# A new order table for a fused attention and channel-mix kernel, with one-bank tiles for the first transposes and the reciprocal as an operation of its own

## The chip, the cores and the metric

The kernel runs on one core of a Trainium2 chip. The core has TensorE (matmuls and transposes), VectorE, ScalarE, GpSimd and SyncE, each with an instruction queue of its own that is worked in order; they wait for one another by semaphores. TensorE writes to PSUM, eight banks here of 128 partitions x 512 float32; the other engines copy from there to SBUF. Transfers are issued here by GpSimd (loads of inputs and weights, which cast float32 to bfloat16 on the way) and by SyncE (stores, and transposes from SBUF to SBUF). The metric is the device time of one execution in microseconds. Before the change the median of three runs is 307.29 us (306.47 to 307.72).

## The reference

Two layers in a row. First an attention with a feature map, for 8 batches of 8 heads, 576 positions and a head size of 64:

```python
def phi(x):
    proj = np.einsum('bhsd,df->bhsf', x, w_phi)                  # 64 -> 128 features
    proj = proj - np.max(np.abs(proj), axis=-1, keepdims=True)
    return np.concatenate([np.exp(proj), np.exp(-proj)], axis=-1)
q_p, k_p = (phi(q), phi(k))
kv = np.einsum('bhsf,bhsd->bhfd', k_p, v)
z = np.sum(k_p, axis=2)
num = np.einsum('bhsf,bhfd->bhsd', q_p, kv)
den = np.einsum('bhsf,bhf->bhs', q_p, z)[..., None] + 1e-06
attn = num / den
```

Then, with the heads side by side as x (8 x 576 x 512), a channel mix of a batch's row with the row before it:

```python
x_prev = np.concatenate([np.zeros((B, 1, D)), x[:, :-1, :]], axis=1)
xk = mu_k * x + (1.0 - mu_k) * x_prev
xr = mu_r * x + (1.0 - mu_r) * x_prev
k = np.maximum(xk @ w_k, 0.0)                                    # 512 -> 1024
v = k * k @ w_v                                                  # 1024 -> 512
r = 1.0 / (1.0 + np.exp(-(xr @ w_r)))
out = r * v
```

## The kernel before

The kernel works in "pairs": two heads of one batch, numbered 0 to 31, four to a batch. Every step of a pair or a batch is an entry in a plan, with a name; a long text, ORDER, says in which order the entries are written into the program. As every engine works in order, this text fixes the order on each engine. An entry may carry the number of its PSUM buffer (`:1`), the engine that does it (`/ACT`), and filler matmuls ahead of it (`+3@0`: three, into buffer 0), which keep TensorE going. Entries that end in `.d` mark the landing of a transfer and write nothing into the program.

```python
ORDER = """
ones ident lv0.0 lv0.0.d:0 lk0.1 lq0.1 lv0.1 dve2 hk hq hk.d:0 lk0.1.d:0 dve3 hq.d:0 lk0.0.d/ACT
lq0.0.d/DVE lk0.2 lq0.2 pt0:2+9@0 wphi wphi.d:0 mus dve1 lv0.2 lk1.0 pb0/DVE pa0/ACT tr0 tp0.0:2+1@0
# ... (some hundred lines)
```

PSUM is shared out as three double buffers P0 to P2 of two banks each and two single ones, M0 and M1:

```python
def fill(n, i):
    t = psum.tile([128, 512], FP, name="ps_f", tag=f"M{i}")
    for _ in range(n):
        nc.tensor.matmul(t, lhsT=ones[:, 0:128], rhs=ones, start=True, stop=True)

def ptile(key, name):
    return psum.tile([128, 2, 512], FP, name=name, tag=f"P{plan.place[key]}")

def motile(key, name):
    return psum.tile([128, 512], FP, name=name, tag=f"M{plan.place[key]}")
```

Queries and keys are loaded by GpSimd (`lk`, `lq`; values: `lv`; weights: `wk`, `wr`, `wv`) and transposed: those of the first two batches (pairs 0 to 7) by TensorE (`pt`, then copies `pa` and `pb`), those of the others by a DMA transpose of SyncE (`tr`).

```python
def pt(b, a):
    def f():
        # ...
        ps = ptile(("P", f"pt{i}"), "ps_pt")
        pb = ps.rearrange("p a x -> p (a x)").bitcast(BF).rearrange("p (a g t) -> p a g t", a=2, t=128)
        st["pb", i] = pb
        for g in range(R):                                        # R = 9
            bk, o = divmod(g, 5)
            nc.tensor.transpose(pb[:, bk, o, :], nat[b][:, a, g * 128:(g + 1) * 128], ident)
    return f

def tr(p0, p1):
    def f():
        # ...
        nc.sync.dma_start_transpose(out=t[:, R * p0:R * p1, :],
                                    in_=nat[b][:, p0:p1, :].rearrange("p a x -> p (a x)"))
    return f
```

A pair n then goes: projections of queries and keys (`qp`, `kp`), the greatest absolute values (`rq`, `rk`: tile `nm`), these split in two bfloat16 parts on GpSimd (`mh`: tile `mhl`), transposed (`mt`, `mc`) and added back by a matmul (`ka`, and in `qt` for queries), exponentials (`ea`, `eb`, `qa`, `qb`), the product of keys and values (`kv`, `kc`), numerator and denominator (`nd`), division (`rd`). The last positions of all pairs of a batch go a way of their own by parts of a batch (`tp`, `rt`, `mhe`: tile `mhlt`, `mte`, `mce`, `kae`, `ekt`, `qte`, `eqe`). The division and what follows:

```python
def rd():
    s["rd"] = small.tile([128, 2, 5], FP, name="rden")
    ndv = s["nd"][:, :, 0:325].rearrange("p b (s e) -> p b s e", e=65)
    nc.vector.reciprocal(s["rd"], ndv[:, :, :, 64])
    s["x"] = mid.tile([128, 10, 64], BF, name="x_sc", bufs=BUFS["x"])
    nc.vector.tensor_tensor(s["x"].rearrange("p (b s) d -> p b s d", b=2), ndv[:, :, :, 0:64],
                            s["rd"].to_broadcast([128, 2, 5, 64]), op=ALU.mult)

def xz():                                                         # pairs 8 to 31
    newx()
    nc.sync.dma_start_transpose(out=xs[:, a, :].rearrange("p (g t) -> p g t", g=5),
                                in_=s["x"].rearrange("p s d -> p (s d)"))

def xu(eng):                                                      # the edge copy
    copy(eng, xs[:, a, 1:64], xs[:, a, 576:639])
    (nc.vector if eng == "DVE" else nc.gpsimd).memset(xs[:, a, 0:1], 0.0)
```

For pairs 0 to 7 TensorE transposes the result instead (`xt`, copies `xe` and `xf`). Then come the difference of neighbours (`df`, on VectorE or GpSimd) and the two mixes (`xa`, `xb`, on VectorE). With the four pairs of a batch b mixed, its channel mix follows: `h` (into 1024), `rl` (relu), `sq` (square), `r` and `th` (the gate), `v` and `ob` (product), `so` (store); the last positions of two batches go together (`he`, `re`, `ve`, ...). The matmuls of `h`, `r` and `v` stand between those of the pairs of later batches.

Of the kernel before, what the change touches and what calls it, by code (L numbers as in the profile page):

```python
# [19 lines left out]
ones ident lv0.0 lv0.0.d:0 lk0.1 lq0.1 lv0.1 dve2 hk hq hk.d:0 lk0.1.d:0 dve3 hq.d:0 lk0.0.d/ACT  # L20
lq0.0.d/DVE lk0.2 lq0.2 pt0:2+9@0 wphi wphi.d:0 mus dve1 lv0.2 lk1.0 pb0/DVE pa0/ACT tr0 tp0.0:2+1@0
rt0.0 mhe0.0 lk0.2.d:0 qp0:1 rq0 lq0.2.d:0 kp0:0 rk0 mte0.0:1+3@0 lq1.0 lq1.0.d:0 lv1.0 mh0
lq0.1.d:0 pt1:1 pa1/DVE mce0.0/ACT kae0.0 lk1.2 lq1.2 lv1.2 pb1/ACT tr1 lq1.2.d:0 qp1:1+2@0 mt0:1
rq1 ekt0.0 mc0/ACT wk.0 pt2:2 ka0 pb2/DVE pa2/ACT kp1:1 rk1 mh1 ea0 pt3:2 pb3/ACT lk1.0.d:0 eb0
pa3/DVE tr3 mt1:1+4@0 mc1/DVE tr2 vc0/POOL wk.1 qp2:2 ka1 ea1 mus.d:0 eb1 rq2 kv0:0 kc0/DVE wr.0
wk.1.d:0 wr.1 lv1.2.d:0 kp2:2+1@0 rk2 wv.0 qt0:0 pt4:1+1@0 lv1.0.d:0 mh2 mt2:1+1@0 qa0 qb0 lk1.2.d:0
pa4/DVE pb4/DVE qte0.0:0 eqe0.0 tp0.1:1 mc2/DVE ka2 tr4 lv0.2.d:0 pt5:0 ea2 rt0.1 mhe0.1
mte0.1:0+1@1 pb5/DVE wv.0.d:0 pa5/DVE eb2 mce0.1/DVE kae0.1+2@1 lv0.1.d:0 ekt0.1 pt6:0 pb6/ACT
pa6/DVE pt7:2 pa7/DVE nd0:1 qt1:0 rd0 pb7/ACT vc1/POOL vc2/POOL vc3/ACT qp3:2 rq3 kp3:1+1@1 wv.1 rk3
mh3 tr6 qa1 qb1 tp0.2:2+3@1 qte0.1:0 tr7 eqe0.1 rt0.2 mhe0.2 kv1:0 kc1/ACT xt0:1 xf0/ACT mt3:0  # L30
mc3/ACT nd1:0 tr5 vc4/POOL xe0/ACT ka3 ea3 eb3 df0/POOL mte0.2:1+1@0 rd1 xt1:0 mce0.2/DVE kae0.2
ekt0.2 tp1.0:0 qte0.2:1 eqe0.2 rt1.0 qp4:1 qt2:2 lk2.0 qa2 qb2 mhe1.0 mte1.0:1 rq4 xa0 kv2:1 kc2/ACT
mce1.0/DVE kae1.0 ekt1.0 vc5/POOL xf1/DVE xb0 qte1.0:1 wr.0.d:0 kp4:2 kv3:1 eqe1.0 kc3/ACT nd2:0 rk4
mh4 mt4:1 rd2 qp5:1 mc4/ACT ka4 rq5 xe1/ACT wk.0.d:0 ea4 eb4 lq2.0 xt2:1 lq2.0.d:0 qp6:0 rq6
df1/POOL xa1 qt3:1+1@0 qa3 kv4:2+1@0 kc4/DVE wk.d xb1 wr.1.d:0 kp5:0 qt4:2+1@0 rk5 qb3 nd3:1 rd3 mh5
xe2/ACT mt5:0+3@0 lk2.0.d:0 tr2.0 xf2/ACT xt3:1 qa4 qb4 mc5/ACT df2/DVE ka5 xe3/ACT xf3/ACT tr2.2
xa2 xb2 wv.1.d:0 ea5 eb5 nd4:2 rd4 df3/POOL xa3 qt5:1 qa5 xb3 kv5:0+3@0 tr2.2.d:0 kp6:2 xt4:1
xf4/ACT xe4/DVE kc5/ACT h0.0:0 h0.1:1 qb5 rl0.0/ACT rl0.1/ACT sq0.0/ACT vc6/POOL vc7/DVE rk6 qp7:1
nd5:0 df4/POOL rq7 mh6 mt6:1 mc6/ACT h0.2:0 rl0.2/ACT qt6:1 qa6 xa4 tr2.0.d:0 wr.d r0.0:1 tr9 xb4
sq0.2/POOL th0.0 tr8 rd5 h0.3:0 qb6 sq0.1/POOL rl0.3/DVE lv2.0 lv2.0.d:0 xt5:1 xf5/DVE xe5/DVE ka6  # L40
kp7:0 h0.4:0 h0.5:1 qp8:1 ea6 df5/POOL eb6 rl0.4/ACT sq0.4/ACT rk7 mh7 sq0.3/ACT kv6:2 rl0.5/DVE
mt7:1 mc7/ACT lk3.0 lq3.0 lv3.0 lk4.0 lq4.0 rq8 lk4.0.d:0 kc6/ACT r0.1:0 th0.1 ka7 ea7 eb7 tr11 tr10
lq3.0.d:0 tp2.0:1 rt2.0 h0.6:1 r0.2:0 rl0.6/DVE sq0.6/ACT th0.2 nd6:2 rd6 h0.7:1 mhe2.0 mte2.0:0
mce2.0/DVE vc8/POOL vc9/POOL kv7:0 kc7/DVE rl0.7/ACT vc10/POOL kae2.0 ekt2.0 qp9:2 rq9 qte2.0:1
xt6:0 sq0.7/POOL qt7:0 lk3.0.d:0 xf6/DVE xe6/DVE eqe2.0 qa7 qb7 kp8:1 rk8 kp9:2 rk9 wv.d sq0.5/POOL
v0.0:0 ob0.0 tr3.0 so0.0 mh8 mt8:1 nd7:0 mc8/ACT ka8 mh9 mt9:0 mc9/ACT xa5 tr3.2 xb5 v0.1:1 rd7
ob0.1 tr3.2.d:0 vc11/ACT ea8 df6/POOL eb8 xa6 xb6 v0.2:0 ob0.2 xt7:1 xe7/ACT xf7/ACT qt8:1 qa8 qb8
df7/DVE xa7 xb7 ka9 lv3.0.d:0 vc12/POOL kv8:0 r0.3:0 tr3.0.d:0 tr13 tr12 lq4.0.d:0 th0.3 v0.3:1
kc8/DVE ob0.3 kp10:0 so0.1 qp10:1 rq10 rk10 ea9 eb9 h1.0:0 h1.1:1 rl1.0/ACT sq1.0/ACT nd8:1 rd8
kv9:2 kc9/ACT h1.2:0 qt9:1 qp11:2 mh10 rq11 rl1.1/ACT xz8 rl1.2/ACT sq1.2/POOL mt10:1 so0.2 mc10/ACT  # L50
sq1.1/POOL h1.3:0 rl1.3/DVE qa9 qb9 r1.0:1 th1.0 sq1.3/POOL kp11:2 rk11 mh11 ka10 ea10 h1.4:0 tr15
eb10 lv4.0 rl1.4/DVE sq1.4/ACT h1.5:1 rl1.5/DVE mt11:0 mc11/DVE so0.3 nd9:1 qp12:0 sq1.5/ACT ka11
xz8.d:0 ea11 eb11 h1.6:0 h1.7:1 vc13/POOL vc14/POOL tr14 vc15/POOL rd9 rq12 xz9 qt10:1 xz9.d:0
rl1.7/DVE rl1.6/DVE lk5.0 kv10:2 kc10/DVE tp3.0:0 sq1.7/POOL rt3.0 qa10 mhe3.0 qb10 r1.1:1 th1.1
he0.0:0 rle0.0/DVE nd10:1 r1.2:1 sq1.6/ACT mte3.0:0 mce3.0/ACT rd10 xz10 xz10.d:0 qt11:2 th1.2
# [12 lines left out]
tp4.0:0 kv15:1 kc15/ACT h2.6:0 sq2.4/ACT rl2.5/DVE rt4.0 mhe4.0 rl2.6/DVE nd14:1 rd14 h2.7:1 qb15
vc20/POOL xa12 sq2.5/POOL lk5.0.d:0 xu13/POOL mte4.0:0 kp16:2 rk16 mce4.0/ACT kp17:1 rk17 kae4.0
mh16 rl2.7/ACT ekt4.0 r2.1:0 r2.2:1 th2.1 mt16:0 mc16/DVE xb12 xz14 df13/DVE nd15:0 so1.2.d:0 rd15  # L70
sq2.6/ACT xz15 sq2.7/ACT lq6.0.d:0 th2.2 mh17 ka16 ea16 xa13 v2.0:0 ob2.0 xb13 tr5.0 tr5.2 tr5.0.d:0
tr20 v2.1:1 eb16 mt17:0 mc17/ACT xz14.d:0 kv16:2 kc16/ACT ob2.1 vc21/POOL vc22/POOL qp18:0 rq18 ka17
ea17 qte4.0:1 xu14/POOL eb17 kp18:2 rk18 v2.2:0 eqe4.0 tr5.2.d:0 tr23 qp19:1 lk6.0.d:0 xz15.d:0
xu15/POOL df14/POOL xa14 qt16:0 qa16 ob2.2 r2.3:1 th2.3 mh18 v2.3:0 rq19 qb16 df15/POOL mt18:1
mc18/ACT kv17:1 so2.0 kc17/ACT xb14 ka18 ea18 eb18 qt17:0 qa17 qb17 nd16:1 xa15 xb15 h3.0:1 ob2.3
rd16 xz16 h3.1:0 rl3.0/DVE sq3.0/POOL so2.3 qp20:1 kp19:2 h3.2:1 rl3.2/ACT so2.2 rl3.1/DVE rk19
so2.2.d:0 r3.0:0 rq20 h3.3:1 th3.0 mh19 sq3.1/ACT sq3.2/POOL vc23/ACT rl3.3/ACT mt19:0 mc19/DVE
nd17:1 r3.1:0 th3.1 sq3.3/ACT so2.0.d:0 tr22 qt18:0 rd17 xz17 xz17.d:0 xz16.d:0 xu16/POOL qa18 qb18
ka19 ea19 df16/POOL xa16 kv18:1 kc18/DVE h3.4:0 rl3.4/DVE lk7.0 tr21 tp5.0:1 rt5.0 h3.5:1 sq3.4/DVE
# [78 lines left out]
def kernel(  # L158
# [813 lines left out]
```

## Time and profile before

| | value |
|---|---|
| median time | 307.29 us |
| span of the profiled execution | 304.2 us |
| TensorE busy | 278.4 us |
| VectorE busy | 240.3 us |
| ScalarE busy | 223.3 us |
| GpSimd busy | 127.4 us |
| moved by DMA | 38.18 MB |

Busy means that an instruction of the engine ran; for TensorE, whose matmuls are pipelined, the ends are modelled, so a busy TensorE may still run below its peak. The share of a group of lines in the chain of waits is that of the path which, followed back from the last instruction, set the end. Names in the lines are those of the tiles: `ps_pt` the PSUM of the first transposes, `qkT` the transposed queries and keys, `x_sc` the divided result and `xs` its transpose, `nm` the negated maxima, `diff` the difference of neighbours. `<-` after a bracket names what the idle time before an instruction ended with.

### The profile page before, as it was taken

The numbers are of one execution on the slowest core, as the hardware profiler recorded it, in microseconds if no ns is written. First come the engines' busy times: TensorE is split into PE (matmuls) and PEld (weight loads), VectorE is DVE, ScalarE is ACT, GpSimd is POOL, SyncE is SP. The second block draws the span as 40 slices with busy tenths as digits, with TensorE's granted clock in tenths as the row PEclk, the third lists the DMA queues.
The fourth block names the chain that finished last, engine by engine and source line by source line (L and its number), as shares of the span: only waits on it lengthen the run. The fifth ranks groups of instructions, "written<-read, shape, count | busy, mean of one in ns | idle before, by whom it ended". The sixth has DMA issues, their size and how long they took to land.

```text
span 304.2 us, 9054 instructions
## 1 busy us (share of the span) xinstructions
PE 278.4 (92%) x3765; PEld 158.4 (52%) x3813; DVE 240.3 (79%) x369; ACT 223.3 (73%) x408; POOL 127.4 (42%) x261
## 2 busy tenths in 40 slices
PE   6688798999899999969999997999999999999993
PEld 2456465565456655534555654454556655554541
DVE  5776789979978999667978988799869888777331
ACT  3397899998689897855888884898797878923410
POOL 7763533696047346653443714353034403400400
PEclk9999989999999999998999999999999999999999
DMA  8999957399989957996957898913924364233125
GB/s 152 204 209 207 169 83 105 59 194 206 194 174 128 148 124 131 197 200 113 177 110 107 145 125 157 162 47 61 187 60 69 11 93 94 58 74 71 39 58 116
DMA packets 66137, 38.18 MB, mean 126 GB/s; under 512 B 47024, under 2 KB 60720, under 8 KB 66096
## 3 DMA queue, kind: packets, MB, share of 16 engines
q1 hardware_dynamic: 51280, 20.82, 39.4%
q0 software_dynamic: 14672, 16.48, 35.1%
q8 instruction: 30, 0.49, 0.7%
q10 hardware_dynamic: 144, 0.29, 0.3%
q14 instruction: 11, 0.09, 0.1%
HBM read 33.62 MB, written 9.44 MB: 142 GB/s over the span
## 4 chain that ended last, share of the span: by engine, by line
PE 61%; DVE 18%; DMA 7%; ACT 6%; issue 3%; POOL 2%; SPq 1%; DVEq 0%; POOLq 0%
PE ps_v L812 14%; PE ps_h L779 13%; PE ps_r L798 7%; PE ps_nd L656 5%; DMA xs<-x_sc 4%; PE ps_kv L635 4%; DVE nm L565 4%; DVE nm L560 3%; DVE xk L706 2%; PE ps_ve L896 2%; ACT q L620 2%; PE ps_he L866 2%; DVE xr L706 2%; PE ps_q L548 2%; PE ps_k L598 2%
## 5 line engine op out<-in xcount | busy, mean ns | idle before, releaser
L620 ACT ACTIVATE q<-ps_qT 128x512 bf16<-128x512 f32 x128 | 67.1, 622 | 3.0 <-PE ps_qT L612 2.8
L575 ACT ACTIVATE k<-ps_k 128x1024 bf16<-128x1024 f32 x64 | 62.9, 1038 | 5.6 <-PE ps_k L598 4.3
L779 PE MATMUL ps_h<-xk,wk_bf 128*128 128x512 bf16 x237 | 60.8, 379 | 1.3 <-issue 0.3
L812 PE MATMUL ps_v<-wv_bf,kk 128*128 128x512 bf16 x243 | 58.2, 379 | 1.0 <-issue 0.3
L565 DVE TENSOR_REDUCE nm<-ps_q 128x8 f32<-128x1024 f32 x32 | 38.7, 1218 | 4.3 <-PE ps_q L548 4.1
L560 DVE TENSOR_REDUCE nm<-ps_k 128x8 f32<-128x1024 f32 x32 | 38.8, 1217 | 3.8 <-PE ps_k L548 3.8
L812 PEld LDWEIGHTS <-kk 128*128 128x128 bf16 x256 | 23.9, 98 | 28.8 <-issue 1.9
L211 POOL TENSOR_TENSOR kk<-krelu 128x512 bf16<-128x512 bf16 x23 | 23.9, 1047 | 35.4 <-DVE krelu L205 21.7
L779 PEld LDWEIGHTS <-wk_bf 128*128 128x128 bf16 x256 | 22.5, 97 | 25.2 <-issue 2.3
L584 POOL CAST mhl<-nm 128x16 bf16<-128x16 f32 x32 | 8.0, 250 | 64.1 <-DVE nm L560 64.0
L798 PE MATMUL ps_r<-wr_bf,xr 128*128 128x512 bf16 x118 | 32.9, 394 | 1.2 <-issue 0.5
L804 ACT ACTIVATE rt<-ps_r 128x512 bf16<-128x512 f32 x32 | 19.5, 609 | 18.0 <-PE ps_r L798 15.7
L700 POOL TENSOR_TENSOR diff<-xs 128x576 bf16<-128x576 bf16 x21 | 28.0, 1336 | 7.6 <-DVE xs L682 2.8
L203 ACT ACTIVATE krelu<-ps_h 128x512 bf16<-128x512 f32 x39 | 23.2, 611 | 10.1 <-PE ps_h L779 8.3
L706 DVE SCALAR_TENSOR_TENSOR xk<-diff,mu_k_t,xs 128x576 bf16<-128x576 bf16 x32 | 28.5, 892 | 1.3 <-POOL diff L700 1.0
L818 DVE SCALAR_TENSOR_TENSOR ob<-rt,ps_v 128x512 f32<-128x512 bf16 x32 | 21.8, 682 | 8.7 <-PE ps_v L812 4.2
L666 DVE TENSOR_TENSOR x_sc<-ps_nd,rden 128x640 bf16<-128x640 f32 x32 | 26.4, 825 | 1.1
L706 DVE SCALAR_TENSOR_TENSOR xr<-diff,mu_r_t,xs 128x576 bf16<-128x576 bf16 x32 | 26.9, 840 | 0.0
L548 PEld LDWEIGHTS <-qkT 64*128 64x128 bf16 x512 | 17.6, 94 | 12.0 <-issue 9.7
L635 PE MATMUL ps_kv<-v,k 64*128 64x65 bf16 x1024 | 22.8, 192 | 0.6 <-ACT q L620 0.4
L635 PEld LDWEIGHTS <-k 64*128 64x128 bf16 x1024 | 19.9, 95 | 5.1 <-issue 3.8
L205 DVE TENSOR_SCALAR krelu<-ps_h 128x512 bf16<-128x512 f32 x25 | 17.1, 688 | 6.6 <-PE ps_h L779 6.0
(99 smaller groups left out, 467.5 us busy)
## 6 DMA issues: line engine op xcount, KB each, us to landing
out_dram<-ob SPq DMA_DIRECT2D x72, 128.0 KB, 2.4
nat<-in_k_dram POOLq DMA_DIRECT2D x6, 576.0 KB, 8.6
nat<-in_q_dram POOLq DMA_DIRECT2D x6, 576.0 KB, 8.9
vt<-in_v_dram POOLq DMA_DIRECT2D x6, 576.0 KB, 9.6
wk_bf<-in_moe_w_k_dram POOLq DMA_DIRECT2D x2, 512.0 KB, 10.8
wv_bf<-in_moe_w_v_dram POOLq DMA_DIRECT2D x2, 512.0 KB, 12.3
nat<-in_k_dram POOLq DMA_DIRECT2D x3, 288.0 KB, 7.4
nat<-in_q_dram POOLq DMA_DIRECT2D x3, 288.0 KB, 7.3
```

The costliest lines, as they stand in the source:

```text
L211: (nc.vector if eng == "DVE" else nc.gpsimd).tensor_tensor(out_, in_, in_, op=ALU.mult)
L560: nc.vector.tensor_reduce(s["nm"][:, 0, :], s["k"].rearrange("p a (g f) -> p (a g) f", f=128), axis=AX.X, op=ALU.max, apply_absolute_value ...
L565: nc.vector.tensor_reduce(s["nm"][:, 1, :], s["q"].rearrange("p a (g f) -> p (a g) f", f=128), axis=AX.X, op=ALU.max, apply_absolute_value ...
L575: nc.scalar.activation(s[f"k{pn}"], s["k"].rearrange("p a (g f) -> p (a g) f", f=128), AF.Exp, scale=(1.0 if pn == 0 else -1.0))
L620: nc.scalar.activation(t[:, h, :].rearrange("f (g a p) -> f g a p", g=4, a=2), s["qT"].rearrange("f a (g h p) -> f h g a p", g=4, h=2)[:, ...
L635: nc.tensor.matmul(ps[:, hh, pn * 65:(pn + 1) * 65], lhsT=s[f"k{pn}"][r, c, :], rhs=vb[r, a, 2 * g + par, :], start=(pn == 0 and c == 0), ...
L666: nc.vector.tensor_tensor(s["x"].rearrange("p (b s) d -> p b s d", b=2), ndv[:, :, :, 0:64], s["rd"].to_broadcast([128, 2, 5, 64]), op=ALU ...
L700: (nc.vector if eng == "DVE" else nc.gpsimd).tensor_tensor(s["d"], xs[:, a, 64:64 + S], xs[:, a, 0:S], op=ALU.subtract)
L706: nc.vector.scalar_tensor_tensor(out=t[:, a, (b % 2) * S:(b % 2 + 1) * S], in0=s["d"], scalar=mu[:, a:a + 1], in1=xs[:, a, 0:S], op0=ALU.m ...
L779: nc.tensor.matmul(ps, lhsT=wk_bf[:, c, fc * 128:(fc + 1) * 128], rhs=xkt[bp][:, c, m0:m0 + 512], start=(c == 0), stop=(c == NDC - 1))
L798: nc.tensor.matmul(ps, lhsT=xrt[bp][:, c, m0 + ci * 128:m0 + (ci + 1) * 128], rhs=wr_bf[:, c, :], start=(c == 0), stop=(c == NDC - 1))
L812: nc.tensor.matmul(ps, lhsT=s["kk"][:, fc, ci * 128:(ci + 1) * 128], rhs=wv_bf[:, fc, :], start=(fc == 0), stop=(fc == NFC - 1))
```

## The change

Four things are changed. ORDER is written anew, all of it; in the new one the loads are placed with regard to all DMA transposes, so that the two do not meet on the DMA engines in the plan; many relus, squares, copies and differences get another engine than before. The first transposes of a pair are split: the first five of nine blocks go to one single buffer and the other four to another, each with its own copy, so that they need no double buffer. The reciprocal of the denominator becomes an entry of its own (`ra`), so that the order can place it apart from the multiplication. And the edge copy `xu` may be on ScalarE, filler matmuls may use the double buffers, and the weights' loads no longer follow the last load of values in the plan.

```diff
 ORDER = """
-ones ident lv0.0 lv0.0.d:0 lk0.1 lq0.1 lv0.1 dve2 hk hq hk.d:0 lk0.1.d:0 dve3 hq.d:0 lk0.0.d/ACT
-lq0.0.d/DVE lk0.2 lq0.2 pt0:2+9@0 wphi wphi.d:0 mus dve1 lv0.2 lk1.0 pb0/DVE pa0/ACT tr0 tp0.0:2+1@0
 # ... (all lines)
+ones hk hq ident dve2 hk.d hq.d wphi wphi.d lv0.0 lv0.0.d lk0.1 lk0.1.d mus mus.d lq0.1 lq0.1.d dve3
+lv0.1 lv0.1.d lk0.2 lk0.2.d lk0.0.d/DVE lq0.0.d/ACT lq0.2 lq0.2.d pt0.0:0+9@0 lv0.2 lv0.2.d pt0.1:1
+pa0/DVE pb0/ACT tr0 lk1.0 lk1.0.d dve1 tp0.0:0+1@2 kp0:1 rt0.0 qp0:2 rq0 mhe0.0 lq1.0 lq1.0.d
 # ... (all lines)
@@ fill
-        t = psum.tile([128, 512], FP, name="ps_f", tag=f"M{i}")
+        if i < 2:
+            t = psum.tile([128, 512], FP, name="ps_f", tag=f"M{i}")
+        else:
+            t = psum.tile([128, 2, 512], FP, name="ps_g", tag=f"P{i - 2}")[:, 0, :]
@@ the first transposes
-        def pt(b, a):
-            def f():
-
+        def pt(b, a, bk):
+            def f():
                 i = NP * b + a
                 get(qkT, b, inp, [128, NP * R, 128], BF, "qkT")
-                ps = ptile(("P", f"pt{i}"), "ps_pt")
-                pb = ps.rearrange("p a x -> p (a x)").bitcast(BF).rearrange("p (a g t) -> p a g t", a=2, t=128)
-                st["pb", i] = pb
-                for g in range(R):
-                    bk, o = divmod(g, 5)
-                    nc.tensor.transpose(pb[:, bk, o, :], nat[b][:, a, g * 128:(g + 1) * 128], ident)
+                ps = motile(("mo", f"pt{i}.{bk}"), "ps_pt")
+                st["pb", i, bk] = pb = ps.bitcast(BF).rearrange("p (g t) -> p g t", t=128)
+                for g in range(5 * bk, min(R, 5 * bk + 5)):
+                    nc.tensor.transpose(pb[:, g - 5 * bk, :], nat[b][:, a, g * 128:(g + 1) * 128], ident)
@@ the division
+        def ra():
+            s["rd"] = small.tile([128, 2, 5], FP, name="rden")
+            s["ndv"] = s["nd"][:, :, 0:325].rearrange("p b (s e) -> p b s e", e=65)
+            nc.vector.reciprocal(s["rd"], s["ndv"][:, :, :, 64])
+
         def rd():
-            s["rd"] = small.tile([128, 2, 5], FP, name="rden")
-            ndv = s["nd"][:, :, 0:325].rearrange("p b (s e) -> p b s e", e=65)
-            nc.vector.reciprocal(s["rd"], ndv[:, :, :, 64])
             s["x"] = mid.tile([128, 10, 64], BF, name="x_sc", bufs=BUFS["x"])
-            nc.vector.tensor_tensor(s["x"].rearrange("p (b s) d -> p b s d", b=2), ndv[:, :, :, 0:64],
+            nc.vector.tensor_tensor(s["x"].rearrange("p (b s) d -> p b s d", b=2), s["ndv"][:, :, :, 0:64],
                                     s["rd"].to_broadcast([128, 2, 5, 64]), op=ALU.mult)
@@ the edge copy
             copy(eng, xs[:, a, 1:64], xs[:, a, 576:639])
-            (nc.vector if eng == "DVE" else nc.gpsimd).memset(xs[:, a, 0:1], 0.0)
+            if eng == "ACT":
+                nc.scalar.copy(xs[:, a, 0:1], zero)
+            else:
+                (nc.vector if eng == "DVE" else nc.gpsimd).memset(xs[:, a, 0:1], 0.0)
@@ loads of the weights, in the plan
-            op(f"{nm_}.{i}", "POOL", 0.75, i - 8, ldw(...), ["lv1.2"], chain="ld")
+            op(f"{nm_}.{i}", "POOL", 0.75, i - 8, ldw(...), ["ident"], chain="ld")
```

## The prediction

> **What bounds the kernel now.** I read the page first (busy shares, then the chain), then the busy time by stretch, then the waits of TensorE stretch by stretch, then the single transfers where TensorE had stood still. The page's shares and chain:
>
> ```profile
> PE 278.4 (92%) x3765; PEld 158.4 (52%) x3813; DVE 240.3 (79%) x369; ACT 223.3 (73%) x408; POOL 127.4 (42%) x261
> ...
> PE 61%; DVE 18%; DMA 7%; ACT 6%; issue 3%; POOL 2%; SPq 1%; DVEq 0%; POOLq 0%
> ```
>
> TensorE has work for 278.4 of 304.2 us, so no reordering can win more than the 25.8 us in which it stands still, plus what the busy figure hides in modelled ends. The chain says the same: 61% of the way to the end is TensorE itself. VectorE at 79% is the second engine. The average hides where the idle time lies, so here is the same by stretch (length, then busy TensorE, weight load, VectorE, ScalarE, GpSimd, then granted clock):
>
> ```profile
> 0.00:52.00 52.00, 40.60 (x674) 25.83 (x680) 38.96 (x75) 38.03 (x74) 28.60 (x64) 0.97 1.00 164
> 52.00:118.00 66.00, 64.00 (x925) 37.31 (x935) 59.34 (x84) 55.82 (x104) 35.15 (x66) 1.00 0.94 150
> 118.00:145.00 27.00, 23.86 (x315) 12.64 (x319) 19.95 (x29) 18.13 (x32) 14.06 (x29) 0.94 1.01 164
> 145.00:275.00 130.00, 125.86 (x1733) 71.09 (x1753) 111.16 (x166) 102.97 (x185) 46.45 (x100) 1.00 0.61 102
> 275.00:304.00 29.00, 24.07 (x131) 11.48 (x131) 10.93 (x19) 8.31 (x14) 3.18 (x3) 0.98 0.34 73
> ```
>
> TensorE stands still for 11.4 us in the start, 2.0 in the second stretch, 3.1 in the short third one (with a clock of 0.94 besides, worth another 27 x 0.06 = 1.6), 4.1 in the long fourth one, and 4.9 at the end, which is the last stores. Two of these have a cause that the change touches.
>
> First, the stretch at 118 us. Its transfers, against those of a stretch with no loads (200 to 235 us), median us to landing last:
>
> ```profile
> nat<-in_k_dram POOLq DMA_DIRECT2D x1, 576.0 KB, 16.4
> xs<-x_sc SPq DMA_TRANSPOSE x3, 11.0
> ```
>
> ```profile
> xs<-x_sc SPq DMA_TRANSPOSE x5, 2.6
> qkT<-nat SPq DMA_TRANSPOSE x2, 4.8
> ```
>
> The same transpose takes 2.6 us alone and 11.0 beside loads. What it does to TensorE is in the timeline:
>
> ```profile
> 131.54 0.23 POOL L199 COPY xs<-xs 128x63 bf16<-128x63 bf16 x1 [2.80 <-DMA xs<-x_sc]
> 131.71 0.10 POOL L682 MEMSET xs<- 128x1 bf16 x1
> 131.88 1.27 POOL L700 TENSOR_TENSOR diff<-xs 128x576 bf16<-128x576 bf16 x1
> 133.10 0.18 POOL L470 CAST mhlt<-me 128x4 bf16<-128x4 f32 x1
> ```
>
> ```profile
> 134.53 0.23 PE L476 MATMUL ps_me<-ident,mhlt 128*128 128x128 bf16 x1 [2.44 <-POOL mhlt L471]
> ```
>
> GpSimd works in order: it waits for the late transpose, then makes `diff`, and only then the `mhlt` that TensorE waits for, 2.44 us.
>
> Second, the start. The first transposes and their two copies out of PSUM:
>
> ```profile
> 6.66 0.23 DVE L248 CAST wph<-wph_f 128x128 bf16<-128x128 f32 x1 [1.53 <-DMA wph_f<-in_w_phi_dram]
> 6.81 0.42 DVE L199 COPY qkT<-ps_pt 128x512 bf16<-128x512 bf16 x1
> 7.26 0.69 ACT L197 COPY qkT<-ps_pt 128x640 bf16<-128x640 bf16 x1 [1.75 <-DVE qkT L199]
> 8.00 0.10 PEld L455 LDWEIGHTS <-qkT 64*128 64x128 bf16 x2 [1.78 <-ACT qkT L197]
> ```
>
> Both halves are in one two-bank tile, and ScalarE starts its half only when VectorE has done its own; VectorE in turn first waits for the cast of `wph`. The list of waits has 5.0 us in 4 cases of ScalarE waiting so for VectorE, and 2.4 in 2 of the reverse.
>
> **What the Trainium skill says.** (1) "DMA: Bandwidth & Descriptors", section "Issuing engines are not separate DMA queues": transfers of all issuing engines run on the same 16 DMA engines and interleave. The trace agrees: 2.6 against 11.0 us. (2) The same page, "Rules for kernel authors": a transpose beside ordinary DMAs needs nothing. So keeping loads away is a matter of time alone, and nothing but the order enforces it. (3) "SBUF — State Buffer", under its diagram of ports: VectorE and GpSimd share a port pair which one holds for a whole instruction. The trace fits: the mix operations `xk` and `xr` (128x576) have means of 892 and 840 ns, and many single ones in the timeline 0.72 to 0.82. (4) "TensorE: Matmul & The Clock Gate", Part 1: an idle array loses its full clock. Here the clock is 0.94 in just the stretch with the longest idle piece.
>
> **The change, part by part.**
>
> *Two tiles for a transpose.* For the first 8 pairs, the 5+4 transposes go to two one-bank tiles. In the built program none of the 16 copies waits for the other engine any more. First pair by hand: the casts end at 5.5 us as now; five transposes take about 0.35 of the present 0.65, so VectorE copies at about 6.0 to 6.5 (0.49) and, as the new order has the `wph` cast after it, casts at 6.66 to 6.9; ScalarE copies its four blocks at 6.3 to 6.9 (0.59). The first projection starts at about 6.95, not 8.00: 1.05 us. The next two pairs have the same cross wait (1.17 us each), partly behind loads, which still land at the rate of the DMA engines (164 GB/s over the start, all engines busy). I give 1.5 us for these and for less crowding of the three two-bank buffers, so 2.5 in the start, of the 3.8 us that TensorE waits there for copies of `qkT`.
>
> *Order of loads.* Counted in TensorE work (each operation at its spacing in the trace, 252 us in all, unchanged: 39 filler matmuls before, 40 after), the old order puts loads of three tensors just ahead of the transposes of pairs 13 and 14, with 7.7 and 5.3 us of work up to their use. In the new one the use of pair 13 is 4.6 behind its transpose, but no load was issued in the 10 before. Where loads remain near (pairs 9, 10, 16, 21, 22), the use stands 9.2 to 17.6 us off; most uncrowded ones 2.4 to 5. That is an order made with the true cost of a collision. The idle 3.1 and the slow clock's 1.6 of the third stretch are at stake, 4.7 together; I take 3.0, since some collision will fall elsewhere. From the other 2.0 + 4.1 us of idle I take 0.5.
>
> *Work moved between engines.* Counting the engine marks in both tables, times the means by shape: GpSimd loses 8 squares (1.05), 4 `diff` (1.34), 8 copies of `v` (0.74) and 10 edge copies with their memset (0.35): 8.4 + 5.3 + 5.9 + 3.5 = 23.1 us. VectorE gains 12 squares (6.5), 4 `diff` (2.0), 5 copies of `v` (2.2), 4 edge copies (0.9), 7 of `kv` (3.0), 7 of `mT` (1.5) and 3 + 3 out of `ps_x` (1.9), and gives 10 relus (6.9) to ScalarE: +11 us. ScalarE comes out about even: +6.1 for relus, +2.0 for `v`, +2.5 for edge copies, -2.6, -2.6, -1.9 and -2.6 for squares, `kv`, `mT` and `ps_x`. VectorE then has about 251 us, or 249 if a fifth less GpSimd work takes some of the port waits with it. In the fourth stretch it was at 111.2 of 130; about 5 us more makes it 89%. That lies beside TensorE's work, but with queues: I charge 1.5 us.
>
> *Reciprocal split off.* The same two instructions (0.22 and 0.83 us, 32 each); only the place of the first may differ. 0.
>
> Sum: -2.5 - 3.0 - 0.5 + 1.5 = -4.5, and 307.3 - 4.5 = 302.8 us.
>
> **The rivals.** *VectorE becomes the bound.* For: +11 us on an engine with 59.3 of 66 us busy in the second stretch, and 13 of the 24 edge copies now stand on VectorE or ScalarE, which wait in order for a transpose where mostly GpSimd did (33.5 us of waits, nearly harmless at 42%). Against: the engine still has more slack than TensorE. This would give back everything: about 308. *The collisions only move.* For: nothing enforces the plan, since loads go when GpSimd comes to them; pairs 9 and 10 are issued right behind two loads. Against: their uses are 10.6 and 13.4 us of work away. That leaves the start's gain alone: about 305. *A denser order throughout.* The start's 11.4 us shrink by 5 and the middle's 9.2 by 5, with little lost on VectorE: about 298. For: the table is new in all its parts; against: TensorE is at 97% in the second and fourth stretch already.
>
> **Range and chances.** The middle is 302.8; the rivals stand at 298, 305 and 308, so 297.5 to 308.0 should hold it 8 times in 10. Over 2% faster means below 301.1, a little under the middle: 0.36. Slower by over 2% means above 313.4, which takes a misfit of the order that no rival here explains: 0.08. Within 2%: 0.56.
>
> **What would show it.** Right: the first projection at about 7 us; no wait of a `ps_pt` copy for the other engine; transposes of `x_sc` late only where their use is late too; TensorE idle in the middle (52 to 275) at 6 us or less, from 9.2; VectorE at 247 to 252 us busy, GpSimd near 104. Wrong: new waits of VectorE or ScalarE for `xs<-x_sc` of over 5 us together, TensorE waiting for VectorE's `nm`, or the first MoE matmul no earlier than the present 51.9 us.

## The result and the profile after

The changed kernel takes 292.19 us (median of four runs, 291.41 to 293.83), the kernel before 307.00 beside it. The ratio is 0.953, with a 95% interval of 0.949 to 0.957: 14.8 us less, where the prediction had 4.5. It lies below the range.

The page of the kernel after, busy shares and chain:

```profile
PE 272.8 (94%) x3765; PEld 157.2 (54%) x3814; DVE 242.8 (84%) x409; ACT 222.8 (77%) x409; POOL 108.8 (38%) x221
...
PE 65%; DVE 9%; DMA 6%; ACT 4%; issue 2%; POOL 1%; DVEq 0%; SPq 0%; ACTq 0%
```

TensorE ran the same 3765 recorded matmuls in 5.6 us less of busy time (272.8 for 278.4) and stood still for 9.1 us less (289.5 - 272.8 = 16.7, for 25.8). VectorE's part of the chain halved, from 18% to 9%, although its busy time grew. So the other engines hold TensorE up less: in the list of its waits VectorE has 4.7 us (before 6.9), ScalarE 1.7 (5.0) and GpSimd 0.7 (4.7). By stretch, with the columns of before (length, busy TensorE, weight load, VectorE, ScalarE, GpSimd, granted clock, DMA share, GB/s):

```profile
0.00:52.00 52.00, 45.21 (x732) 28.00 (x740) 46.29 (x91) 43.53 (x84) 33.58 (x72) 1.00 1.02 174
52.00:118.00 66.00, 64.18 (x987) 37.95 (x999) 59.87 (x92) 56.21 (x103) 30.30 (x53) 1.00 1.12 162
118.00:145.00 27.00, 26.66 (x348) 14.63 (x351) 24.10 (x38) 23.54 (x44) 11.21 (x26) 1.00 1.05 155
145.00:275.00 130.00, 127.23 (x1661) 72.56 (x1684) 109.06 (x186) 97.80 (x178) 33.73 (x70) 1.00 0.57 99
275.00:289.50 14.50, 9.47 (x43) 4.11 (x42) 3.44 (x5) 1.75 (x3) 0.00 (x0) 0.94 0.40 92
```

The idle time is 6.8 us in the start (11.4 before), 1.8 + 0.3 + 2.8 = 4.9 from 52 to 275 us (9.2 before) and 5.0 in the tail (4.9 before). The clock is full in all stretches but the tail; before, it was 0.97 in the start and 0.94 in the third. The third stretch, where before TensorE stood still for 3.1 us, now loses 0.3.

The start, from the timeline (start, duration, instruction, idle time before it and what ended it):

```profile
6.11 0.49 DVE L199 COPY qkT<-ps_pt 128x640 bf16<-128x640 bf16 x1 [0.55 <-PE ps_pt L334]
6.33 0.59 ACT L197 COPY qkT<-ps_pt 128x512 bf16<-128x512 bf16 x1 [0.93 <-PE ps_pt L334]
6.52 0.22 DVE L249 CAST wph<-wph_f 128x128 bf16<-128x128 f32 x1
6.80 0.23 PE L456 MATMUL ps_e<-wph,qkT 64*128 64x128 bf16 x2 [0.28 <-DVE wph L249]
```

Each copy now waits for TensorE alone, the two overlap, and the first projection starts at 6.80 us instead of 8.00. By the first matmul of the channel mix the lead has grown to 7.8 us. First the line of before, then that of after:

```profile
51.92 1.03 PE L779 MATMUL ps_h<-xk,wk_bf 128*128 128x512 bf16 x3
```

```profile
44.14 1.02 PE L786 MATMUL ps_h<-xk,wk_bf 128*128 128x512 bf16 x4
```

TensorE had about the same work behind it at that point (an estimate: 30.2 us by the spacing of its operations, before 30.9; the new order has one `kv` and one `xt` less ahead of it and one filler matmul more). The other 7 us come between there and the end.

The waits for the transposes of `x_sc` (total us, times, longest), after:

```profile
POOL xs L199 <- DMA xs<-x_sc: 15.2, 4, 4.7
...
DVE xs L199 <- DMA xs<-x_sc: 2.3, 3, 1.0
```

GpSimd had 33.5 us in 12 such waits before. Yet the transposes themselves did not become quicker. The times from issue to landing of all 24, first of before, then of after:

```profile
DMA to landing us min/median/max: 2.6/3.5/13.4
```

```profile
DMA to landing us min/median/max: 2.4/3.8/12.1
```

The new order doesn't keep loads and transposes apart: in the trace of after the transposes of pairs 9 and 10 still take 12.1 and 11.8 us beside loads, as the plan let them, and those of pairs 12, 14 and 23, which the prediction did not list among those with loads near, 7.6, 7.8 and 7.1 us. It puts the late ones where their use is far off.

### The profile page after: what moved, and what is told of

It reads as the page before. It is cut to its first block, busy times and chain, and to the rows that moved or that the text cites. A ratio compares the mean times of both kernels' runs of the same rounds, so it can differ in the third digit from the quotient of the medians.

```text
span 289.5 us, 9053 instructions
## 1 busy us (share of the span) xinstructions
PE 272.8 (94%) x3765; PEld 157.2 (54%) x3814; DVE 242.8 (84%) x409; ACT 222.8 (77%) x409; POOL 108.8 (38%) x221
## 4 chain that ended last, share of the span: by engine, by line
PE 65%; DVE 9%; DMA 6%; ACT 4%; issue 2%; POOL 1%; DVEq 0%; SPq 0%; ACTq 0%
PE ps_h L786 16%; PE ps_v L819 15%; PE ps_r L805 7%; DMA xs<-x_sc 6%; PE ps_nd L657 5%; PE ps_kv L636 4%; PE ps_ve L903 2%; PE ps_he L873 2%; ACT k L576 2%; PE ps_qT L607 2%; PE ps_k L549 2%; PE ps_k L599 2%; DVE nm L561 2%; PE ps_q L549 2%; PE ps_qT L613 1%
## 5 line engine op out<-in xcount | busy, mean ns | idle before, releaser
L203 ACT ACTIVATE krelu<-ps_h 128x512 bf16<-128x512 f32 x46 | 27.9, 611 | 8.9 <-PE ps_h L786 7.2
L811 ACT ACTIVATE rt<-ps_r 128x512 bf16<-128x512 f32 x32 | 19.3, 608 | 18.8 <-PE ps_r L805 14.4
L805 PE MATMUL ps_r<-wr_bf,xr 128*128 128x512 bf16 x117 | 30.7, 379 | 1.2 <-issue 0.5
L706 POOL TENSOR_TENSOR diff<-xs 128x576 bf16<-128x576 bf16 x17 | 22.7, 1334 | 22.8 <-DVE xs L688 17.1
L712 DVE SCALAR_TENSOR_TENSOR xk<-diff,mu_k_t,xs 128x576 bf16<-128x576 bf16 x32 | 26.5, 829 | 1.2 <-POOL diff L706 1.0
L211 POOL TENSOR_TENSOR kk<-krelu 128x512 bf16<-128x512 bf16 x16 | 17.4, 1088 | 18.0 <-ACT krelu L203 11.0
L636 PE MATMUL ps_kv<-v,k 64*128 64x65 bf16 x1024 | 22.2, 190 | 1.3 <-ACT q L621 1.0
L657 PE MATMUL ps_nd<-kv,q 128*128 128x65 bf16 x512 | 21.4, 193 | 0.0
```

What stands on the lines that cost most here:

```text
L203: nc.scalar.activation(out_, in_, AF.Relu, scale=HALF)
L636: nc.tensor.matmul(ps[:, hh, pn * 65:(pn + 1) * 65], lhsT=s[f"k{pn}"][r, c, :], rhs=vb[r, a, 2 * g + par, :], start=(pn == 0 and c == 0), ...
L657: nc.tensor.matmul(ps[:, bk, o * 65:(o + 1) * 65], lhsT=tail if sl < 2 else s[f"q{pn}"][:, h, G * 128:(G + 1) * 128], rhs=s["kv"][:, h, pn ...
L712: nc.vector.scalar_tensor_tensor(out=t[:, a, (b % 2) * S:(b % 2 + 1) * S], in0=s["d"], scalar=mu[:, a:a + 1], in1=xs[:, a, 0:S], op0=ALU.m ...
L805: nc.tensor.matmul(ps, lhsT=xrt[bp][:, c, m0 + ci * 128:m0 + (ci + 1) * 128], rhs=wr_bf[:, c, :], start=(c == 0), stop=(c == NDC - 1))
```

## The experiments

The theory to test was the prediction's own: the gain is (a) a start without the cross waits, through the one-bank tiles, and (b) loads that no longer hold up a transpose that is needed soon. The rivals: (c) the loads hardly matter, and the gain is the new order as a whole, or (d) the new share-out of work between the engines. Fifteen runs followed. A saving in us below is one minus the ratio to the kernel before, times 307. In the later runs the first loads landed 1 to 3 us later than in the first two traces (the keys of the third pair at 11.1 to 13.2 us instead of 10.4), so kernels are compared by ratio, and traces by differences within one trace.

### Without the loads of batches 2 to 7

Two kernels leave out the loads of queries, keys and values of batches 2 to 7, so that those batches compute on what batches 0 and 1 left in the buffers; nothing else differs. The same edit was made in before (b_noload) and in after (a_noload):

```diff
+                if b >= 2:
+                    nat[b] = nat[b - 2]
+                    return
 ... and in the load of the values
+            if b >= 2:
+                vt[b] = vt[b - 2]
+                return
```

> The kernel before without the loads of queries, keys and values of batches 2 to 7 (it takes those of batches 0 and 1 again), so no DMA transpose meets a load. If the middle's 7.0 us come from collisions of transposes with loads: about 300. If they come from the order and the engines: 304 to 307.

> The changed kernel without those same loads. If the change took the cost of the collisions away: within 1.5 us of 292.2. If collisions still cost it (transposes of 12 us are still in its trace): 287 to 289.

Measured: b_noload 300.48 us, ratio 0.978 (0.972 to 0.984); a_noload 291.94 us, ratio 0.951 (0.946 to 0.956). The loads cost the old order some 6.8 us. They cost the new one nothing that the intervals can show: 0.951 against 0.953 with them, and 0.960 (0.953 to 0.966) in a second run of after.

But b_noload takes away more than the traffic: it also takes GpSimd's part in it, the issue of the loads and its waits for free buffers. So a third kernel, b_tiny, keeps every load of before in its place and cuts it to 16 of 576 columns:

```diff
+                w = 16 if b >= 2 else X
-                nc.gpsimd.dma_start(out=t[:, a0:a1, o:o + X], in_=heads(src, b, a0, a1))
+                nc.gpsimd.dma_start(out=t[:, a0:a1, o:o + w], in_=heads(src, b, a0, a1)[:, :, 0:w])
```

> The kernel before with the loads of queries, keys and values of batches 2 to 7 cut to 16 of 576 columns (they write into the tiles of batches 0 and 1, whose data all later batches take): GpSimd issues them at the same places and waits for the same buffers, but hardly anything is moved. If the 7 us that came from leaving the loads out are collisions on the DMA engines: again near 300.5, ratio 0.975 to 0.985. If they are GpSimd's time and its waits for buffers: 0.995 or more.

Measured: 300.47 us, ratio 0.980 (0.974 to 0.986), a saving of 6.0 us. That is within the intervals of b_noload's 6.8, so what the loads cost is nearly all traffic. The longest landing of a transpose of `x_sc` falls from 13.4 us to 4.9, the median from 3.5 to 2.6. Its busy time by stretch:

```profile
118.00:145.00 27.00, 26.63 (x364) 14.51 (x363) 23.77 (x34) 21.75 (x38) 17.76 (x35) 1.00 0.59 91
145.00:275.00 130.00, 129.30 (x1736) 71.57 (x1735) 109.98 (x168) 102.29 (x185) 43.91 (x95) 1.00 0.47 85
```

The idle time is 0.4 instead of 3.1 us in the third stretch, with the full clock, and 0.7 instead of 4.1 in the fourth. As the order of before is untouched, the same operations can be timed in both traces. Take the reciprocals of the denominators as marks: from pair 14 to pair 16 it is 22.4 us before (131.3 to 153.7) and 17.9 in b_tiny; from pair 18 to pair 20, 22.2 before (165.4 to 187.6) and 20.0. Elsewhere between pairs 2 and 30 no two neighbouring marks (every second pair) differ by over 1.1 us. So there are two places that cost, 4.5 and 2.2 us, and the prediction knew only the first. The second, in the timeline of before:

```profile
183.62 0.24 POOL L199 COPY xs<-xs 128x63 bf16<-128x63 bf16 x1 [7.40 <-DMA xs<-x_sc]
183.93 0.46 DVE L700 TENSOR_TENSOR diff<-xs 128x576 bf16<-128x576 bf16 x1 [2.51 <-POOL xs L682]
...
187.75 0.22 PE L589 MATMUL ps_m<-ident,mhl 128*128 128x128 bf16 x1 [1.55 <-DVE ob L818]
```

GpSimd waits 7.40 us for the late transpose, VectorE 2.51 us for GpSimd, and TensorE then 1.55 us for a product `ob` that VectorE, now late, had yet to make. The late transfer reaches TensorE through two engines that each work in order, and under the name of a third operation.

### The loads moved

b_newloads is before with the loads of batches 2 to 7 placed as in after, each behind the same GpSimd step `mh` (only `lv7` stays earlier); a_oldloads is after with the loads where before has them (three had to come later, behind the operations that free their buffers: `lv5` behind `vc15`, `lk6` behind `tr4.2`, `lv6` behind `vc19`). One of the loads moved, of many:

```diff
 b_newloads
-lk3.0 lq3.0 lv3.0 lk4.0 lq4.0 rq8 lk4.0.d:0
+h1.2:0 qt9:1 qp11:2 mh10 lk4.0 lk4.0.d rq11
 a_oldloads
-mh10 xf6/DVE df6/DVE mt10:1 lk4.0 lk4.0.d qt8:2
+lq3.0 lq3.0.d lv3.0 lv3.0.d lk4.0 lk4.0.d lq4.0 lq4.0.d
```

> The order and engines of the kernel before, but the loads of batches 2 to 7 stand behind those steps of GpSimd behind which the changed kernel has them. Without its loads this kernel won 7 us, so the collisions cost 7. If the place of the loads alone avoids them: ratio 0.978 to 0.985. If the distance from a transpose to its use is what avoids the cost (the old order keeps it short): 0.99 to 1.0.

> The reverse: the changed kernel with the loads of batches 2 to 7 behind the steps of GpSimd behind which the kernel before had them. Place of the loads decides: ratio to the kernel before 0.965 to 0.98, and waits of VectorE or ScalarE for the transpose of x_sc appear. Distance decides: within 0.005 of the changed kernel's 0.953.

Measured: b_newloads 319.42 us, ratio 1.042 (1.034 to 1.050); a_oldloads 309.34 us, ratio 1.007 (1.005 to 1.010). Both are slower, and in a_oldloads not by later transposes of `x_sc`: they take at most 10.3 us there, in after up to 12.1. GpSimd around 117 us, and TensorE after it:

```profile
116.70 0.74 POOL L319 DMA_DIRECT2D nat<-in_k_dram  x1 [10.39 <-DMA qkT<-nat]
117.43 0.21 POOL L584 CAST mhl<-nm 128x16 bf16<-128x16 f32 x1
117.73 0.22 POOL L585 TENSOR_TENSOR mhl<-nm,mhl 128x16 bf16<-128x16 f32 x1
```

```profile
118.00 0.29 PE L589 MATMUL ps_m<-ident,mhl 128*128 128x128 bf16 x1 [6.27 <-POOL mhl L585]
```

A load of `nat` overwrites a buffer that a DMA transpose of an earlier batch has yet to read; that transpose is issued only at 108.89 us and lands 7.2 us later, beside a load of values. The load stands at the head of GpSimd's queue for 10.39 us, behind it stands `mhl`, 0.4 us of work, and TensorE waits 6.27 us for that.

In b_newloads TensorE also waits for `mhl`, 9.7 us in seven pieces, but behind other things. No load is held by its buffer there; GpSimd stands before a late transpose (here) or before values that have not landed (6.16 us, then 4.65 of TensorE):

```profile
104.10 0.24 POOL L200 COPY xs<-xs 128x63 bf16<-128x63 bf16 x1 [5.24 <-DMA xs<-x_sc]
```

```profile
105.00 0.23 PE L594 MATMUL ps_m<-ident,mhl 128*128 128x128 bf16 x1 [1.71 <-POOL mhl L590]
```

GpSimd's waits for `xs<-x_sc` are 39.9 us in this run, before 33.5: the places that after has for the loads do not avoid the collisions in the old order. So the two runs don't tell collisions from the rest, as they were meant to: a_oldloads mixes a held load with a transpose that traffic slows, b_newloads collisions with late values. They show two ties of the loads to the order. A place is good only with the uses that stand around it, and a load that comes before its buffer is free blocks the engine that issues it.

### The start and the tiles

startold keeps before's order, tiles and engines up to the numerator of pair 4 and goes on in the new order; startnew has the new order up to `kp6` (about 39 us) and then goes on in the old one. sn_tiny is startnew with the loads cut as in b_tiny.

```diff
 startold
-ORDER = new
+ORDER = old up to nd4, then what is left, in the sequence of new
 startnew
-ORDER = old
+ORDER = new up to kp6, then what is left, in the sequence of old
```

> The order, the two-bank tiles of the first transposes and the engine marks of the kernel before up to the numerator of pair 4 (the last step ahead of the first MoE matmul), all else from the changed kernel. If the gain is two separate ones, as the milestones of the two traces say (first MoE matmul 7.8 us earlier, another 7.0 us won between it and the end), this kernel keeps the second alone: 307.0 - 7.0 = 300.0 us. If the early start is what feeds the later gain (more ready work ahead of TensorE), it stays near 307. If the start is worth nothing by itself, it is near 292.

> The reverse: order, one-bank tiles and marks of the changed kernel up to the key projection of pair 6 (just ahead of the first MoE matmul), then the order and marks of the kernel before. Two separate gains: 307.0 - 7.8 = 299.2 us. If the later part of the old order can't use the earlier start (it stands still at the loads as before): over 303.

> The new start with the rest of the old order, with the same loads cut to 16 columns. The new start alone won 3 us of the 7.8 by which its first MoE matmul is earlier. If the collisions in the old rest eat the other 4 to 5: 307 - 7 - 7.8 = 292 us, ratio 0.95 to 0.96. If the old rest can't use an earlier start whatever the transfers do: 0.965 to 0.975.

Measured: startold 299.57 us, ratio 0.976 (0.970 to 0.982); startnew 304.00 us, 0.990 (0.987 to 0.993); sn_tiny 297.21 us, 0.969 (0.964 to 0.973). The new start alone saves 3.1 us, the new rest alone 7.4. Start and taken-away traffic add up: 3.1 + 6.0 = 9.1, and 9.6 measured together, which is the same within the intervals.

The tiles by themselves: b_split is before with the two parts of each first transpose in tiles of their own (the second in a single buffer), and the cast of `wph` moved behind the first copy. The rest of the order stays:

```diff
-lq0.0.d/DVE lk0.2 lq0.2 pt0:2+9@0 wphi wphi.d:0 mus dve1 lv0.2 lk1.0 pb0/DVE pa0/ACT tr0
+lq0.0.d/DVE lk0.2 lq0.2 pt0.0:2+9@0 pt0.1:0 wphi wphi.d:0 mus lv0.2 lk1.0 pb0/DVE dve1 pa0/ACT tr0
```

> The kernel before with the second four blocks of each first transpose in a single buffer of its own (the first five stay in the double buffer), so that no copy waits for the other engine, and with the cast of wph behind VectorE's copy of the first pair: the start's step of the prediction by itself, 2.5 us of the 7.8. Ratio 0.990 to 0.994 if that step was sized right; 0.975 to 0.98 if the tiles are all of the start's gain; 1.0 if the earlier copies are only waited for elsewhere.

Measured: 308.27 us, ratio 1.002 (0.998 to 1.005). The cross waits are gone and the first projection starts at 6.94 us, as foretold, and nothing is won. What TensorE does with the lead, in the timeline of b_split:

```profile
12.46 0.40 PE L336 MATMUL ps_pt<-ident,nat 128*128 128x128 bf16 x4 [1.22 <-DMA nat<-in_k_dram]
13.96 0.45 PE L336 MATMUL ps_pt<-ident,nat 128*128 128x128 bf16 x5 [1.09 <-DMA nat<-in_q_dram]
```

It has finished what stands ahead of the transposes of the third pair at about 11.2 us, over 1 us earlier than before, stands there for 1.22 and 1.09 us until their loads have landed, and the lead is gone. The profiled execution of b_split was a slow one (311.0 us, median 308.27), so only its start is read here. These loads landed about 2 us later than in the trace of before, where TensorE found them in place at 12.43 us; b_tiny, which has before's start and ran on the same chip as b_split, is the fairer comparison:

```profile
13.26 0.45 PE L339 MATMUL ps_pt<-ident,nat 128*128 128x128 bf16 x5 [0.49 <-DMA nat<-in_q_dram]
```

There the old start too stands before the queries of the third pair, so a lead of 1 us had nothing to win. Whether some of it would stay where the loads land as early as in the first trace was not tested. After has other work at this place: its first transpose of the third pair comes at 14.60 us.

Then the reverse: a_twobank is after's order with the old two-bank tiles. The nine transposes of a pair then need one of the three double buffers at a time when the new order has given them away; so `nd0` had to go behind `pb4`, `kp4` behind `eb3`, `qt3` behind `pb6`, `qp5` behind `qb3` and `kp5` behind `kc3`:

```diff
-ekt0.2 pt4.1:0 qa1 nd0:0 pa4/DVE mh2 pb4/DVE tr4
+qa1 pa4/DVE mh2 pb4/DVE nd0:0 tr4
-xf1/DVE kp4:2 eb3 kc2/DVE pt7.0:0 df1/POOL
+xf1/DVE eb3 kp4:0 kc2/DVE df1/POOL
```

> The changed kernel with the two-bank tiles of before for the first transposes: the nine transposes of a pair stand together, its two copies wait for each other again, and five steps (numerator 0, query transform 3, key projections 4 and 5, query projection 5) had to be pushed behind a copy or an exponential, because all three double buffers are taken at their old place. If the tiles only matter by letting the new order stand as it does: 2 to 4 us slower than the changed kernel run beside it. If the tiles are worth nothing: within 1 us. If they are the whole of the start's gain: 7 us.

Measured: 309.16 us, ratio 1.007 (1.004 to 1.010), 15 us more than after on the same chip (294.02). The reciprocal of pair 4 comes at 62.2 us, in that run of after at 46.8; from pair 3 to the end the lag stays at 15 us. From the stretches and TensorE's waits in a_twobank:

```profile
16.00:32.00 16.00, 10.93 (x182) 7.19 (x174) 8.76 (x16) 10.17 (x21) 7.74 (x17) 0.89 1.19 207
32.00:44.00 12.00, 8.19 (x155) 6.04 (x156) 8.23 (x16) 6.49 (x12) 4.72 (x8) 0.86 0.90 147
44.00:52.00 8.00, 4.81 (x79) 3.55 (x78) 3.17 (x3) 5.82 (x12) 0.12 (x1) 0.50 0.67 151
52.00:62.00 10.00, 9.31 (x135) 5.35 (x133) 9.41 (x13) 8.48 (x18) 2.76 (x7) 0.89 0.01 2
```

```profile
PE ps_q L550 <- ACT q L622: 2.8, 1, 2.8
...
PE ps_k L550 <- ACT k L577: 2.0, 1, 2.0
```

TensorE waits for a double buffer that ScalarE has not yet emptied, and between 44 and 52 us the granted clock is 0.50. This agrees with the Trainium skill, "TensorE: Matmul & The Clock Gate", Part 1, which puts the gated clock at half the full one. The slow clock is a large part of the loss: over the four stretches it takes away up to 16 x 0.11 + 12 x 0.14 + 8 x 0.50 + 10 x 0.11 = 8.5 us of TensorE's time, an upper bound, as TensorE idles in part of it. In that run of after the clock is 1.00 throughout. So the tiles don't save the time of a copy. They leave the double buffers free, and the new start can stand on that; without them come waits, and after the waits half the clock. The five moves were made by hand where the buffers required them; an order planned anew for two-bank tiles was not tried and might lose less than 15 us.

### The engines

b_newengines is before's order with after's choice of engine for each square, relu, difference and copy (173 of 322 entries differ); a_oldengines is the reverse. Five of the entries, from several lines:

```diff
 b_newengines
-rl0.5/DVE sq0.1/POOL df3/POOL kc4/DVE mc6/ACT
+rl0.5/ACT sq0.1/DVE df3/DVE kc4/ACT mc6/DVE
 a_oldengines
-rl0.5/ACT sq0.1/DVE df3/DVE kc4/ACT mc6/DVE
+rl0.5/DVE sq0.1/POOL df3/POOL kc4/DVE mc6/ACT
```

> The order of the kernel before with the engines of the changed kernel for relus, squares, differences, edge copies and copies. If less work on GpSimd is what made the middle faster: 0.98 or less. If the marks only belong to their order: 1.0 or slower, to 1.02.

> The changed order with the engines of the kernel before for the same kinds of steps. If the new marks are worth a part of the gain by themselves: 0.97 or more. If the order alone is: 0.955 to 0.965.

Measured: b_newengines 355.33 us, ratio 1.159 (1.151 to 1.166); a_oldengines 312.48 us, ratio 1.018 (1.010 to 1.025). Rival (d) falls as a cause by itself: alone, the new share-out costs 49 us, though GpSimd then has only 105.7 us of work. TensorE waits 25.7 us for VectorE and 21.8 for ScalarE in b_newengines, before 6.9 and 5.0: steps now stand in the queue of an engine that has other work at their place. Nor does the new order keep its gain without the share-out (a_oldengines). Each order depends on its own, and what is called the order below includes it.

### The reciprocal

a_rajoin is after with each reciprocal put back beside its multiplication:

```diff
-eqe0.2 ra1 mh3 rd1
+eqe0.2 mh3 ra1 rd1
```

> The changed kernel with the reciprocal put back directly ahead of its multiplication. All theories: no difference, within 0.004 of 0.953.

Measured: 294.11 us, ratio 0.959 (0.953 to 0.964). It overlaps both runs of after: no effect, as predicted.

### What is left

new_nd8_tiny has the new order up to the numerator of pair 8 (about 78 us), then the old one, with the loads cut; after_again is after once more on the same chip.

```diff
-ORDER = new
+ORDER = new up to nd8, then what is left, in the sequence of old
```

> Order and engines of the changed kernel up to the numerator of pair 8 (about 78 us), the rest of the order of before, loads of batches 2 to 7 cut to 16 columns so that no collision is in it. With the new order up to 39 us alone this was 0.969. If the missing 5 us to the changed kernel's 0.953 lie in the stretch between 39 and 78 us: 0.955 to 0.96. If they lie behind it: still 0.967 to 0.971.

> The changed kernel itself on the chip of these runs, for comparison: 0.949 to 0.957.

Measured: new_nd8_tiny 295.78 us, ratio 0.965 (0.960 to 0.970); after_again 294.02 us, 0.960 (0.953 to 0.966). Rival (c) in its strong form, that the loads hardly matter, falls; a part of it stays: sn_tiny saves 9.6 us, new_nd8_tiny 10.8, after 12.4 (this run) to 14.4 (the first). So 2.8 to 4.8 us are the order itself, with intervals of 1.3 to 1.9 us to each side.

The traces show better than these ratios where they lie. Behind the numerator of pair 8 the old and the new order leave TensorE the same work. From the reciprocal of that pair to the end of the last product it takes 214.7 us in before, 209.3 in b_tiny and in sn_tiny, 208.9 and 207.6 in the second and first run of after, and 207.1 in a_noload. So behind pair 8 the new order with all loads does what the old one does almost without loads, and 0.4 to 1.7 us better. (In new_nd8_tiny it is 208.3, but the joint of its two orders has put two `h` ahead of the mark.) Up to pair 3 sn_tiny and after have the same order; from there to pair 8 it is 44.3 us in sn_tiny and 42.2 in both runs of after. So 2.0 us lie in this stretch. The two runs of after differ by 1.7 us before pair 3, and the keys and queries of the third pair landed 1.4 us apart in them.

## Why the prediction was wrong

The direction and nearly all of its signs were right; the sum was too small by 8 to 10 us, in several terms. The steps that failed are the size of the collisions (3.5 us foretold, 6.0 measured), the charge for VectorE (1.5 us, nothing seen), and the lack of any term for a denser order and the clock that comes with it (2.8 to 4.8 us). The term for the tiles had nearly the right size by a mechanism that failed.

*Two tiles, -2.5.* The sign came as written (first projection at 6.80 us, foretold 6.95; no copy waits for the other engine), but the step from the sign to the time failed: b_split has the same 1 us lead and saves nothing, since TensorE runs into loads that land no sooner (in that run later than in the first traces). The prediction had seen that ("partly behind loads") and counted the time all the same. The start as a whole saves 3.1 us by startnew, close to the 2.5 by luck, for the reason is another: the tiles free the double buffers, and the order written on that fills the time until the loads have landed. With two-bank tiles, and five steps moved for them, the new order loses its whole gain (a_twobank).

*Order of loads, -3.0 and -0.5.* This is the term that was sized worst among those with a number: 3.5 foretold, 6.0 measured by b_tiny, which takes the traffic away. That the new order saves nearly all of it follows from a_noload. Two choices failed. "I take 3.0, since some collision will fall elsewhere": the first place gave all of its 4.5 us in b_tiny (foretold at stake: 4.7), and the collisions that remain in after cost little (0.5 to 1.8 us behind pair 8, against a_noload). And the idle time of the fourth stretch, 4.1 us, was put down at 0.5 as having no cause that the change touches. It held the same cause, 2.2 us from pair 18 to pair 20. In the list of waits it stands as TensorE waiting 1.6 us for `ob` of VectorE, and was not followed back to the transpose two steps behind it.

*VectorE's work, +1.5.* The charge for a fuller VectorE is nowhere to be seen (TensorE waits 4.7 us for it, before 6.9), and the 11 us were too many: 242.8 us busy, not 247 to 252. For the squares the prediction multiplied a mean that a few long cases had raised. The squares on VectorE (duration min/median/max in ns), before and after:

```profile
L211 DVE TENSOR_TENSOR kk<-krelu x18: 415/426/1493, 164.4 to 283.2; 128x512 bf16<-128x512 bf16 x18
```

```profile
L211 DVE TENSOR_TENSOR kk<-krelu x29: 414/418/455, 49.8 to 273.0; 128x512 bf16<-128x512 bf16 x29
```

The mean before, 549 ns, came from five long squares of the 18 (686 to 1493 ns). In after none is long: 29 squares take 12.1 us where 18 took 9.7, so eleven more cost 2.4 us and not 6. All five long ones stood beside copies or differences of GpSimd, but six of the short ones stood beside GpSimd instructions too; the cause was not tested. The other 4 us of the overestimate were not traced. GpSimd has 108.8 us (foretold 104).

*Reciprocal, 0.* Right.

*The order as such.* No term stood for it; measured are 2.8 to 4.8 us. The third rival, a denser order throughout, had it ("about 298"), and came nearest, with 5 + 5 us of idle time; measured are 4.6 + 4.3. What it lacked is TensorE's busy time, which fell by 5.6 us. The prediction named that reserve ("what the busy figure hides in modelled ends") and gave it no number. The granted clock alone holds 1.6 us in the start (52 x 0.03) and 1.6 in the third stretch. This was no accident of one trace: the mean granted clock of before's executions is 0.984 to 0.987, of after's 0.998 and 1.000, which is worth up to about 4 us. Idle TensorE was paid for twice. The argument against this rival, "TensorE is at 97% in the second and fourth stretch already", was true, but 3% of the fourth stretch are 4.1 us, and the time could be won in the two other stretches as well.

Of the signs for right, all but VectorE's and GpSimd's busy times were seen; of those for wrong, none (VectorE and ScalarE wait 3.0 us for `x_sc` together, TensorE 0.9 us for `nm`, before 1.2). In sum: 9.6 us of the start and the collisions (3.1 and 6.0 by themselves), and 2.8 to 4.8 of the order with its share-out make up the 12.4 to 14.4 us. Of the latter, 2.0 have a place (pairs 3 to 8) but no single cause that a run isolates.

## What to carry to other kernels

Follow each wait of the bounding engine back through every engine that works in order until a transfer or real work is reached: a late transfer can stand in the list as a short wait for something else. A faster first step is worth only as much as the next arrival allows, and a smaller buffer is worth what it lets the order do. Loads, buffers, engines and order fit each other: to move one of them alone cost up to 16% here.

## What the runs showed of the hardware

- With two or three cast loads in flight at its issue, the small transpose from SBUF to SBUF landed 6.0 to 13.4 us later (before and after), with one 2.6 to 7.8, and with the loads cut to 16 columns 2.6 (median of b_tiny). The Trainium skill, "DMA: Bandwidth & Descriptors", "Rules for kernel authors", says that such a transpose needs nothing beside ordinary transfers; it speaks of the data. In time the old order paid 6.0 us of 307 for it.
- A load whose buffer is not free holds the engine that issues it, not only its own transfer: 10.39 us of GpSimd, and 6.27 us of TensorE behind it (a_oldloads).
- A stretch with 3.2 us of idle TensorE in 8 us ran at a clock of 0.50, and the 10 us behind it, with 0.7 us idle, still at 0.89 (a_twobank), so the time lost is more than the idle time that is seen.
